# Which queue carries the first gate weights: exchanging the queues of two opening loads in a fused attention and gated-MLP kernel

## The chip, the cores and the metric

The kernel runs on one core of one Trainium2 chip. The metric is the device time of one execution in microseconds. Kernels are compared only within the same rounds.

## The reference

```python
x = A_x                                   # 2048 rows of 640, bf16
xn = _layernorm(x)
# A: queries xn @ wq, 32 heads of 192, the last 512 keys and values of a cache, softmax, @ wo
s = _A_ref(xn, A_k_cache, A_v_cache, A_wq, A_wo)
# B: sigmoid(xn @ w_gate) * (xn @ w_up), then @ w_down      (640 -> 1536 -> 640)
g = _silu(_B_ref(xn, B_w_gate, B_w_up, B_w_down))
return x + s * g
```

## The kernel before

The kernel computes the gate (B) first. It starts with row tiles of 128 rows: VectorE (DVE) takes the statistics of a tile and centres it, TensorE (PE) turns it through an identity matrix, ScalarE (ACT) copies the turned rows out of PSUM, and PE multiplies them with the first 512 columns of the gate weights, in five chunks of 128 rows of the weights. Seventeen dummy matmuls keep PE busy until the first rows are there (in the profile from 1.05 to 4.86 us; PE's first work on rows starts at 4.70).

These are the loads of the opening. `nc.sync` is SyncE's (SP) queue, `nc.scalar` is ScalarE's; a load that ScalarE issues waits for a fill of two columns (one 4-byte element, 0.06 us in the profile) of its own destination.

```python
def load_x(t, n, eng=nc.sync):
    x = xpool.tile([P, n, D], BF16, name=f"x_sb{n}", bufs=4 if n == 1 else 2)
    if eng is nc.scalar:
        nc.vector.memset(x[:, 0, 0:2], 0.0)
    eng.dma_start(x[:], xf[t * P:(t + n) * P, :].rearrange("(q p) d -> p q d", p=P))
    ...
nc.vector.memset(warm[:], 0.0)
nc.vector.memset(eps_t[:], eps)
load_x(0, 1)                                       # rows 0      SyncE    160 KB
load_x(1, 1, nc.scalar)                            # rows 1      ScalarE  160 KB
load_f(nc.sync, wg_sb, wg_r, 0, 4, 0, 3)           # gate 0 to 2 SyncE    384 KB
load_f(nc.scalar, wg_sb, wg_r, 0, 4, 3, NCD)       # gate 3, 4   ScalarE  256 KB
load_f(nc.sync, wu_sb, wu_r, 0, 4, 0, 3)           # up 0 to 2   SyncE    384 KB
load_x(2, 1)
load_f(nc.sync, wu_sb, wu_r, 0, 4, 3, NCD)
load_x(3, 1)
... # the rest of the weights and rows, all on SyncE
```

And this is the order in which PE consumes them (cut to the matmuls):

```python
dummy(17)
turn_pe(0, 0, 1); turn_pe(0, 1, 3, 2)
tile_half(0, 0, 0, 0, 0, 1)        # rows 0 x gate chunk 0
turn_pe(0, 3, NCD, 1)
tile_half(0, 0, 0, 0, 1, 3)        # rows 0 x gate chunks 1, 2
turn_pe(1, 0, 3)
tile_half(0, 0, 0, 0, 3)           # rows 0 x gate chunks 3, 4
turn_pe(1, 3, NCD, 2)
tile_half(1, 0, 1, 0)              # rows 1 x gate chunks 0 to 4
tile_half(0, 0, 0, 1)              # rows 0 x up: the first use of up weights
```

The softmax here doesn't subtract the row's maximum and nothing guards it: scores larger than these inputs give would overflow.

Of the kernel before, what the change touches and what calls it, by code (L numbers as in the profile page):

```python
# [15 lines left out]
def kernel(  # L16
# [13 lines left out]
    nc = tc.nc  # L30
    P = 128
    H2 = 64

    xf = A_x.flatten_outer_dims()
# [14 lines left out]
    NCD = D // P  # L49
# [36 lines left out]
    wg_r = B_w_gate.rearrange("(c p) f -> p c f", p=P)  # L86
# [56 lines left out]
    with ExitStack() as bctx:  # L143
# [5 lines left out]
        wg_sb = wB.tile([P, NCD, F], BF16, name="wg_sb")  # L149
# [6 lines left out]

        xt = {}

        def load_x(t, n, eng=nc.sync):

            x = xpool.tile([P, n, D], BF16, name=f"x_sb{n}", bufs=4 if n == 1 else 2)
            if eng is nc.scalar:

                nc.vector.memset(x[:, 0, 0:2], 0.0)
            eng.dma_start(x[:], xf[t * P:(t + n) * P, :].rearrange("(q p) d -> p q d", p=P))  # L165
            for i in range(n):
                xt[t + i] = x[:, i, :]

        def load_f(eng, w, r, f0, f1, c0=0, c1=NCD):
            eng.dma_start(w[:, c0:c1, f0 * P:f1 * P], r[:, c0:c1, f0 * P:f1 * P])  # L170

        nc.vector.memset(warm[:], 0.0)
        nc.vector.memset(eps_t[:], eps)
        load_x(0, 1)
        load_x(1, 1, nc.scalar)
        load_f(nc.sync, wg_sb, wg_r, 0, 4, 0, 3)
        load_f(nc.scalar, wg_sb, wg_r, 0, 4, 3, NCD)
        load_f(nc.sync, wu_sb, wu_r, 0, 4, 0, 3)
        load_x(2, 1)
        load_f(nc.sync, wu_sb, wu_r, 0, 4, 3, NCD)  # L180
        load_x(3, 1)
# [489 lines left out]
```

## Time and profile before

| | before |
|---|---|
| device time, median of the first runs | 922.05 us (921.91 to 922.11) |
| span of the profiled run | 920.4 us |
| PE busy | 913.7 us |
| gate chunks 3 and 4: issued, landed | 1.51, 6.90 us |
| PE's wait for them | 0.34 us |

PE's work in order of time (start, us busy, engine, line, operation, tiles, count; in brackets the idle time before it and what ended it).

```profile
5.51 0.39 PE L303 MATMUL bank<-wg_sb,xnT 128*128 128x512 bf16 x1 [0.16 <-ACT xnT L247]
...
6.95 0.59 PE L303 MATMUL bank<-wg_sb,xnT 128*128 128x512 bf16 x2 [0.34 <-DMA wg_sb<-in_B_w_gate_dram]
...
8.57 1.89 PE L303 MATMUL bank<-wu_sb,xnT 128*128 128x512 bf16 x8
```

The first row is gate chunk 0, the second gate chunks 3 and 4 after their wait, the third the first matmul with an up weight. I call the start of that third row (8.57 us) the **length of the opening**.

### The profile page before, as it was taken

The page shows a single profiled execution, that of the slowest core. Times are in us where ns is not written, and L with a number is a line of the kernel's source. Part 1 is how long each engine was busy: PE and PEld are TensorE (multiplying, and loading weights), DVE is VectorE, ACT ScalarE, POOL GpSimd, SP SyncE. Part 2 cuts the span into 40 slices and gives each one's busy share as a digit, 9 for nine tenths or more (in the row PEclk, how much of TensorE's full clock was granted, in tenths as well). Part 3 has the DMA queues.
Part 4 walks back from the last instruction along what each step waited for, and adds up shares of the span by engine and source line. Part 5 has one row for each costly group of instructions (what it writes and reads, how often), then busy time and mean ns, then how long its engine had stood idle before and what let it go on. Part 6 is the DMA issues. An engine that isn't in the chain of part 4 may idle for free.

```text
span 920.4 us, 24974 instructions
## 1 busy us (share of the span) xinstructions
PE 913.7 (99%) x11314; PEld 622.8 (68%) x11333; DVE 492.5 (54%) x987; ACT 303.1 (33%) x334; POOL 126.7 (14%) x147
## 2 busy tenths in 40 slices
PE   9999999999999999999999999999999999999998
PEld 4445455466868686767676777777776767686875
DVE  5452522545646464645555555545564646464667
ACT  4222222255142424233333333242414151515150
POOL 2000100001002000200120011001100111055813
PEclk9999999999999999999999999999999999999999
DMA  9830330116334434342425162516251614246435
GB/s 318 165 44 1 89 86 1 44 62 88 78 63 106 86 56 84 93 99 42 98 80 112 36 105 79 113 29 112 66 106 45 116 61 84 66 96 142 91 72 136
DMA packets 173642, 79.35 MB, mean 86 GB/s; under 512 B 149952, under 2 KB 169616, under 8 KB 173536
## 3 DMA queue, kind: packets, MB, share of 16 engines
q1 hardware_dynamic: 166928, 58.44, 32.1%
q0 software_dynamic: 5040, 17.89, 7.0%
q8 instruction: 88, 1.44, 0.7%
q10 hardware_dynamic: 1568, 1.43, 0.5%
q14 instruction: 18, 0.15, 0.1%
HBM read 39.45 MB, written 2.62 MB: 46 GB/s over the span
## 4 chain that ended last, share of the span: by engine, by line
PE 98%; DMA 1%; DVE 0%; issue 0%; ACT 0%; ACTq 0%; DVEq 0%
PE bank L531 22%; PE bank L457 21%; PE bank L479 19%; PE bank L439 18%; PE bank L261 8%; PE bank L273 6%; PE bank L303 3%; PE bank L405 1%; DMA wg_sb<-in_B_w_gate_dram 1%; PE bank L564 0%; DVE o_sb L509 0%; DVE gate L514 0%; ACT xnT L247 0%; PE bank L245 0%; ACTq L165 0%
## 5 line engine op out<-in xcount | busy, mean ns | idle before, releaser
L443 ACT ACTIVATE E<-bank 128x1024 bf16<-128x1024 f32 x256 | 255.4, 1022 | 456.6 <-PE bank L439 456.3
L457 PE MATMUL bank<-xnT,wq_sb 64*128 64x512 bf16 x1800 | 226.4, 376 | 0.0
L531 PE MATMUL bank<-wo_sb,oT 64*128 64x320 bf16 x2688 | 205.2, 296 | 0.0
L439 PE MATMUL bank<-qT,kT 64*128 64x512 bf16 x1536 | 200.9, 376 | 0.0
L479 PE MATMUL bank<-vbuf,E 64*128 64x193 bf16 x4096 | 195.3, 243 | 0.0
L479 PEld LDWEIGHTS <-E 64*128 64x128 bf16 x4096 | 178.8, 94 | 10.2 <-issue 0.3
L531 PEld LDWEIGHTS <-oT 64*128 64x128 bf16 (+1 forms) x2892 | 163.2, 94 | 30.7 <-issue 0.3
L464 DVE CAST qT<-bank 128x1024 bf16<-128x1024 f32 x90 | 110.2, 1225 | 128.5 <-PE bank L457 128.5
L457 PEld LDWEIGHTS <-wq_sb 64*128 64x128 bf16 x1800 | 106.1, 100 | 87.0 <-issue 0.4
L439 PEld LDWEIGHTS <-kT 64*128 64x128 bf16 x1536 | 88.1, 94 | 73.6 <-issue 0.3
L492 DVE TENSOR_TENSOR o_st<-bank,rden 128x768 bf16<-128x768 f32 x128 | 122.5, 957 | 4.4
L546 DVE TENSOR_TENSOR acc<-bank,acc 128x640 f32<-128x640 f32 x96 | 79.1, 824 | 20.2 <-PE bank L531 20.2
L118 POOL DMA_DIRECT2D vbuf<-in_A_v_cache_dram x28 | 21.1, 755 | 309.2 <-PE bank L479 306.3
L462 DVE COPY seen<-bank 128x2 f32<-128x2 f32 x90 | 14.3, 159 | 79.3 <-PE bank L457 79.3
L491 DVE RECIPROCAL rden<-bank 128x4 f32<-128x4 f32 x128 | 23.4, 183 | 60.6 <-PE bank L479 59.5
L273 PE MATMUL bank<-wd_sb,hT 128*128 128x128 bf16 (+1 forms) x377 | 52.4, 298 | 0.4
L273 PEld LDWEIGHTS <-hT 128*128 128x128 bf16 x384 | 29.7, 98 | 23.1
L261 PE MATMUL bank<-xnT,wg_sb 128*128 128x512 bf16 x176 | 44.5, 379 | 0.2
L261 PE MATMUL bank<-xnT,wu_sb 128*128 128x512 bf16 x177 | 44.6, 379 | 0.2
L267 DVE TENSOR_TENSOR hT<-bank,sig 128x512 bf16<-128x512 f32 x36 | 24.8, 690 | 37.1 <-ACT sig L264 37.1
L264 ACT ACTIVATE sig<-bank 128x512 bf16<-128x512 f32 x36 | 21.5, 597 | 55.8 <-PE bank L261 52.7
L110 POOL COPY k_perm<-k_st 128x768 bf16<-128x768 bf16 x32 | 25.6, 828 | 77.3 <-DMA k_st<-in_A_k_cache_dram 77.3
(52 smaller groups left out, 379.3 us busy)
## 6 DMA issues: line engine op xcount, KB each, us to landing
wo_sb<-in_A_wo_dram SPq DMA_DIRECT2D x7, 960.0 KB, 5.6
wq_sb<-in_A_wq_dram POOLq DMA_DIRECT2D x7, 960.0 KB, 6.0
k_st<-in_A_k_cache_dram POOLq DMA_DIRECT2D x14, 384.0 KB, 5.9
vbuf<-in_A_v_cache_dram POOLq DMA_DIRECT2D x28, 192.0 KB, 4.1
row<-in_A_x_dram SPq DMA_DIRECT2D x16, 160.0 KB, 2.4
oT<-o_st SPq DMA_TRANSPOSE x128, 3.2
x_sb<-in_A_x_dram SPq DMA_DIRECT2D x3, 640.0 KB, 9.4
wd_sb<-in_B_w_down_dram SPq DMA_DIRECT2D x1, 1920.0 KB, 13.9
```

Of the source, the lines that this page charges most:

```text
L110: nc.gpsimd.tensor_copy(kp[:, pr, :, :, i * H2:(i + 1) * H2], kst[:, i, :, :].rearrange("p c (i j) -> p c j i", j=DJ),)
L261: nc.tensor.matmul(bank[k][:, half, 0:r1 - r0], lhsT=w[:, c, f * P:(f + 1) * P], rhs=xnT[:, b, c, r0:r1], start=(c == 0), stop=(c == NCD - 1))
L273: nc.tensor.matmul(wide(k)[:, d0:d1], lhsT=hT[b][:, f, q * P:(q + 1) * P], rhs=wd_sb[:, f, d0:d1], start=(f == 0), stop=(f == NF - 1))
L303: nc.tensor.matmul(bank[k][:, half, :], lhsT=xcT[:, c, t * P:(t + 1) * P], rhs=w[:, c, fg * FT:(fg + 1) * FT], start=(c == 0), stop=(c == ...
L439: nc.tensor.matmul(bank[k][:, i, :], lhsT=kT[r, pr, j, c * P:(c + 1) * P], rhs=q[r, pr * DJ + j, :], start=(j == 0), stop=(j == DJ - 1))
L443: nc.scalar.activation(E[u, pr][:, c, :, :], bank[k][:], AF.Exp, scale=scale_qk)
L457: nc.tensor.matmul(bank[k][:, half, :], lhsT=wq[r, c, col:col + DJ * (P - 1) + 1:DJ], rhs=xnT[r, b, c, :], start=(c == 0 and not second), ...
L464: nc.vector.tensor_copy(qT[u][:, 2 * m:2 * m + 2, :], bank[k][:])
L479: nc.tensor.matmul(o4[:, q, 0:DH + 1], lhsT=e[r, c, h % 2, q * P:(q + 1) * P], rhs=vbuf[r, h, c, 0:DH + 1], start=(turn == 0 and qq == 0 a ...
L492: nc.vector.tensor_tensor(o_st[u][:, :, h * DH:(h + 1) * DH], o4[:, :, 0:DH], rden[:].to_broadcast([P, TQ, DH]), ALU.mult)
L531: nc.tensor.matmul(res[:, half, :], lhsT=oT[u][r, cc, q * P:(q + 1) * P], rhs=wo[r, cc, half * HD:(half + 1) * HD], start=(turn == 0 and c ...
L546: nc.vector.tensor_tensor(cols(acc[:, t, :]), res, cols(acc[:, t, :]), ALU.add)
```

## The change

The intent: the first two row tiles go out one after the other on SyncE's queue, and gate chunks 0 to 2, which are needed first, go out on ScalarE's at the same moment. A fill of 352 columns of their destination holds ScalarE's issue back so that the rows are ahead. Chunks 3 and 4 move to SyncE's queue, in front of the up weights.

```diff
-        def load_x(t, n, eng=nc.sync):
+        def load_x(t, n):
             x = xpool.tile([P, n, D], BF16, name=f"x_sb{n}", bufs=4 if n == 1 else 2)
-            if eng is nc.scalar:
-                nc.vector.memset(x[:, 0, 0:2], 0.0)
-            eng.dma_start(x[:], xf[t * P:(t + n) * P, :].rearrange("(q p) d -> p q d", p=P))
+            nc.sync.dma_start(x[:], xf[t * P:(t + n) * P, :].rearrange("(q p) d -> p q d", p=P))
...
         nc.vector.memset(eps_t[:], eps)
+        nc.vector.memset(wg_sb[:, 0, 0:352], 0.0)
         load_x(0, 1)
-        load_x(1, 1, nc.scalar)
-        load_f(nc.sync, wg_sb, wg_r, 0, 4, 0, 3)
-        load_f(nc.scalar, wg_sb, wg_r, 0, 4, 3, NCD)
+        load_x(1, 1)
+        load_f(nc.scalar, wg_sb, wg_r, 0, 4, 0, 3)
+        load_f(nc.sync, wg_sb, wg_r, 0, 4, 3, NCD)
```

## The prediction

> **What bounds the kernel now.** I read four views, from the whole to the opening. First the busy shares of the page, because a change of the opening can only matter as much as the engine that sets the end lets it.
>
> ```profile
> span 920.4 us, 24974 instructions
> PE 913.7 (99%) x11314; PEld 622.8 (68%) x11333; DVE 492.5 (54%) x987; ACT 303.1 (33%) x334; POOL 126.7 (14%) x147
> ```
>
> TensorE (PE) is busy 913.7 of 920.4 us, so all of the time without matmuls is 6.7 us. Second, the busy time by stretches says where these 6.7 us lie: of the first 20 us PE is busy 18.10, so 1.9 us are idle there; from 20 to 915 us only 0.94 us are idle (80 - 79.53 and 815 - 814.53), and the last 5.4 us hold 3.8 us of the tail (the last rows and their store), which the change leaves alone. The change touches only the first ten microseconds. It can therefore take out at most a part of 1.9 us, and 1.05 of these are the time before the first dummy matmul, which waits for the fill of its own tile and not for a load.
>
> Third, what PE waited for in the first 12 us (engine and line, who released it, total us, times, longest):
>
> ```profile
> PE bank L195 <- DVE x_sb L164: 1.0, 1, 1.0
> PE bank L303 <- DMA wg_sb<-in_B_w_gate_dram: 0.3, 1, 0.3
> PE bank L303 <- ACT xnT L247: 0.3, 2, 0.2
> ```
>
> One wait of 0.34 us (0.3 here, 0.34 in the timeline, between 6.61 and 6.95) is for gate weights; two of about 0.16 us are for turned rows copied out of PSUM by ScalarE (ACT). Fourth, the chain that ended last, in order of time (start, us, what), names which transfer that was:
>
> ```profile
> 1.05 0.43 ACTq L165
> 1.48 0.03 issue
> 1.51 5.39 DMA wg_sb<-in_B_w_gate_dram
> 6.90 0.04 issue
> 6.95 0.59 PE bank L303 x2
> ```
>
> The transfer issued at 1.51 from ScalarE's queue is the second part of the first gate weights (chunks 3 and 4 of 5, 256 KB). It lands 5.39 us after its issue, at 6.90. From there the chain is PE work, apart from two copies by ACT of 0.50 us that hold PE for 0.15 us each. So what this opening pays to the loads is 0.34 us, and the change is aimed at that transfer.
>
> Why does 256 KB take 5.39 us? Queue q1 is SyncE's (SP), q10 is ScalarE's. The DMA view for 2.4 to 5.2 us, and then for 5.2 to 6.6 us (packets, MB, share of 16 engines):
>
> ```profile
> q1 hardware_dynamic: 509, 0.50, 58.8%
> q10 hardware_dynamic: 388, 0.40, 41.3%
> ...
> q1 hardware_dynamic: 412, 0.43, 90.9%
> q10 hardware_dynamic: 28, 0.03, 5.9%
> ```
>
> ScalarE's queue has only the second x row tile (160 KB) and these weights: 416 KB, 416 packets with the completions. By 5.2 us 388 of them have gone; the last 28 need another 1.4 us, beside 412 of SyncE's. The packet records show more: the transfers were served nearly one after the other in order of issue (x0 from 1.6 us, x1 from 2.4, weights 0 to 2 from 2.8, weights 3 and 4 from 4.0, first up weights from 4.7), 14 of the 16 completions of weights 3 and 4 are there by 5.3 us, and two come at 6.46 and 6.54. On two DMA engines the rest of this transfer shared the time with the next transfers of the other queue, the up weights, which nobody needs before 8.57 us. That, not volume, is the wait.
>
> [...]
>
> **The change part by part.** The arithmetic, the order on PE, ACT and POOL after the issues, and the bytes are unchanged. SP issues one transfer more, ACT one less.
>
> *The fill.* The one-column fill of x1 (0.06 us) goes; one of 176 elements comes. From two rows, 1 element at 59 ns and 128 at 165 ns, a further element costs (165-59)/127 = 0.83 ns, so 59 + 175 x 0.83 = about 0.20 us. It starts at 0.95 as its predecessor did and ends at about 1.16. DVE next works at 3.22, so it costs nothing itself. ACT, which began 0.04 us after the end of the old fill (1.01 to 1.05), issues at about 1.20.
>
> *The issues.* Before, SP issues at 0.73, 1.19, 1.66, 2.18: a pace of about 0.47. After: x0 0.73, x1 1.19, weights 3 and 4 at 1.66, first up weights at about 2.15, each later one 0.47 later than before. ACT: weights 0 to 2 at 1.20, as good as the 1.19 they had. In order of issue: x0, x1, weights 0 to 2, weights 3 and 4, up. That is the order of before, with the queues exchanged. That SP's later issues slip costs nothing while the DMA engines have a backlog, and they have: from 2 us on their share is 0.90 to 1.10.
>
> *Weights 3 and 4.* The transfer now stands before the up weights in the same queue[...]. The 14 engines in order say 5.3 us for its last completion; landing was 0.36 us after that before (6.54 to 6.90), so about 5.7. Needed at 6.61: the wait of 0.34 goes, with 0.9 to spare.
>
> *Weights 0 to 2.* Last completion 4.51 before, landing at 1.19 + 3.8 = 5.0; needed at 5.51. If the order of service holds, still about 5.0; 0.5 to spare. It is now these that sit in ScalarE's queue, with weights 3 and 4 behind them in the other: what happened to the one may happen to the other.
>
> *x0 and x1.* x0 is ahead of all as before: landing about 3.15, and the first normalised piece at 4.69, where the 17 dummies (until 4.86) end anyway. x1 landed at 1.05 + 2.4 = 3.45; DVE reaches it at 4.55. Behind x0 in one queue it should land at 3.5 to 3.6: hidden.
>
> *What comes next if PE is 0.34 earlier.* Up weights landed at 1.66 + 5.9 = 7.6, needed at 8.23; their second part at 2.71 + 6.0 = 8.7, needed at about 9.4. x2 landed at 7.98, the last DVE piece before PE's turning is ready at 9.47 (9.15 + 0.32), and PE would ask for it at 10.08 - 0.34 = 9.74: 0.27 to spare. The same bytes stand before x2 as before, so it comes when it came. The two ACT waits stay, as they are between PE and ACT alone.
>
> **Sum:** minus 0.34 us of wait, plus 0 for the fill, plus 0 for the issues: -0.34, all of it carried to the end because nothing between 20 and 915 us waits for a clock other than PE's. For a chance that the exchange bites somewhere I keep 0.30: 922.05 - 0.30 = 921.75 us.
>
> **The rivals.**
> 1. *The late engine changes sides.* Weights 0 to 2, 24 packets on each DMA engine, are alone in ScalarE's queue while SyncE's has weights 3 and 4 and up weights behind. If two engines interleave as before, the landing goes from 5.0 to as much as 6.2. PE then starts the first gate matmul at 6.2 instead of 5.51, does what took from 5.51 to 6.61 (1.10 us) until 7.3, and begins chunk 3 there instead of at 6.95: a loss of about 0.35, so 922.4. For it: the same two queues, the same kind of neighbour. Against: the wait behind these weights was short in the old trace, since all their completions came within 0.5 us (4.03 to 4.51). I give it one in five; break-even is a landing at 5.85.
> 2. *ScalarE's issue overtakes x1.* The two issues are only about 0.01 us apart (1.19 and 1.20), on a fill whose length I worked out. If weights 0 to 2 are served first, x1 comes after them, near 4.5, lands about 4.9, and DVE starts its statistics 0.35 later than 4.55. PE's turn of x1 (6.28, its input ready at 6.03) slips by about 0.1: the gain shrinks to 0.2, so 921.85. For it: the near tie. Against: the fill has plainly been sized to hold this order.
> 3. *Something else was just behind.* If x2 or the up weights come 0.3 later, because SP issues them 0.47 later, PE loses the 0.34 again at 8.2 or 9.7, and the time is 922.05. Against: the backlog of the DMA engines.
>
> **Range and chances.** Some 55% for a gain of 0.2 to 0.5, 25% for about nothing, 20% for a loss of up to 0.4. The three runs of before span 0.20 us, so half of that is to be added at each side. That gives 921.3 to 922.3 as eight in ten. Two per cent would be 18 us, ten times all the idle time of the opening: faster 0.01, same 0.98, slower 0.01.
>
> **What would show it right or wrong.** Right: the waits of PE in the first 12 us have no line for the gate weights; the gate weights from ScalarE land at about 5.0, those from SyncE by 6; the first matmul with an up weight starts near 8.2; PE's busy time in the first 20 us is up by 0.3. Rival 1: a wait of PE for the gate weights before 6.2. Rival 2: DVE waits for x a second time before 5 us. Rival 3: a wait near 8 to 10 us that was not there. Wrong altogether: a difference that doesn't lie in the first 20 us.

What no trace or run of this case shows has been cut out of this text and of three of the expectations below; the cuts are marked. They take no term out of the sum: it came to minus 0.34 us for the wait and 0 for the fill and the issues, of which the author kept 0.30, so 922.05 - 0.30 = 921.75 us. What the argument needs of the cuts stands as follows:

- A landing followed the last of the 16 completions that the packet records have for a transfer: chunks 3 and 4 of the kernel before had 14 by 5.3 us and the last at 6.54, and landed at 6.90; in the changed kernel the last of chunks 0 to 2 came at 4.92, and they landed at 5.33.
- That the fill of 352 columns has 176 elements was an estimate from the warm tile, whose 256 columns show as 128 elements of uint32; the changed kernel's trace has a fill of 176.
- That chunks 3 and 4, in one queue with the up weights, would not share with them was an assumption. The landing of 5.7 us rests on it, and it is not shown.

The records do not name the DMA engine of a packet. Where these texts speak of a late engine, a late completion, one of the 16, is what was seen. And what the expectations call theory or rival is a guess put to the test, not a finding. For the two late completions of the kernel before the records show a little more: from 5.6 us the rest of the transfer goes in two trains, each with a packet every 0.085 us that takes 0.046 us, so that about half of the time was left to other packets.

## The result

The changed kernel took 921.67 us (median of 4, 921.55 to 921.80), the kernel before 921.98 us in the same rounds (median of 4, 921.80 to 922.11). The ratio, the mean time of one kernel's fast runs over that of the other's in the same rounds and so not quite the ratio of these medians, is 0.9997 with a 95% interval of 0.9979 to 1.0014. By the 2% measure it is the same time. The medians differ by 0.31 us. In these rounds and in two further sets of rounds, told below, the interval of the ratio includes 1; that the difference is real rests on the three sets together, in which all 13 runs of the changed kernel took 922.00 us or less, but only 8 of the 34 runs of the kernel before.

The page of the changed kernel, span and busy times:

```profile
span 919.8 us, 24974 instructions
PE 913.4 (99%) x11314; PEld 622.9 (68%) x11333; DVE 492.9 (54%) x987; ACT 303.1 (33%) x334; POOL 126.7 (14%) x147
```

PE does the same work. The span is 0.6 us shorter in this profile: half of that is idle time of PE (6.4 us instead of 6.7), the other half is its busy time. What PE waited for in the first 12 us (engine, line, releaser, total us, times, longest):

```profile
PE bank L194 <- DVE warm L169: 1.0, 1, 1.0
PE bank L302 <- DMA wg_sb<-in_B_w_gate_dram: 0.2, 1, 0.2
PE bank L302 <- ACT xnT L246: 0.2, 1, 0.2
```

There is still a line for gate weights, but it is another wait. The chain that ended last, in order of time, names the transfer:

```profile
1.00 0.20 DVE wg_sb L172
1.20 0.02 issue
1.22 4.11 DMA wg_sb<-in_B_w_gate_dram
5.33 0.04 issue
5.37 0.38 PE bank L302
```

The fill ends at 1.20, ScalarE issues chunks 0 to 2 at 1.22, and they land 4.11 us later, at 5.33. PE, whose other input was ready, starts the first gate matmul on them. Chunks 3 and 4 are no longer in the chain. The DMA view for 2.4 to 5.2 us shows ScalarE's queue (q10) with all of its 400 packets gone; in the view for 5.2 to 6.6 us SyncE's queue is the only one with data:

```profile
q1 hardware_dynamic: 460, 0.47, 55.8%
q10 hardware_dynamic: 400, 0.39, 45.4%
...
q1 hardware_dynamic: 478, 0.49, 104.6%
```

The 28 packets that were late before have no counterpart in ScalarE's queue. For chunks 3 and 4, now in SyncE's, the view can't tell, since it doesn't separate the transfers of one queue. Counted in order in the packet records, 14 of their 16 completions are there by 5.39 us and two come at 5.61 and 5.88, so a shorter tail seems to be left. PE's work in order of time:

```profile
5.37 0.38 PE L302 MATMUL bank<-wg_sb,xnT 128*128 128x512 bf16 x1 [0.20 <-DMA wg_sb<-in_B_w_gate_dram]
...
6.33 0.61 PE L302 MATMUL bank<-wg_sb,xnT 128*128 128x512 bf16 x2
...
7.04 1.25 PE L302 MATMUL bank<-wg_sb,xnT 128*128 128x512 bf16 x5
...
8.13 1.89 PE L302 MATMUL bank<-wu_sb,xnT 128*128 128x512 bf16 x8
```

The opening is 8.13 us long instead of 8.57, 0.44 less. Chunk 0 starts 0.14 earlier. From there to chunks 3 and 4 (the second row) it takes 0.96 us instead of 1.44, which is 0.48 less, more than the 0.34 us that the view put down as idle. The ends of PE's instructions are modelled: here chunks 3 and 4 start 0.21 us after the turn in front of them (6.12 to 6.33), while that turn is still shown busy. Before, the same turn started at 6.28, so chunks 3 and 4 could have started at 6.49, and the wait until 6.95 was worth 0.46 us. From chunks 3 and 4 to the up weights it takes 1.80 instead of 1.62: a part is given back. PE is now early enough that the rows of the second tile, which ACT copies out of PSUM from 6.49 to 6.98, come just before the matmuls that read them (7.04, the third row). So 0.14 + 0.48 - 0.18 makes the 0.44.

### The profile page after: what moved, and what is told of

It is laid out like the page before. It is cut to its first block, busy times and chain, and to the rows that moved or that the text cites. A ratio compares the mean times of both kernels' runs of the same rounds, so it can differ in the third digit from the quotient of the medians.

```text
span 919.8 us, 24974 instructions
## 1 busy us (share of the span) xinstructions
PE 913.4 (99%) x11314; PEld 622.9 (68%) x11333; DVE 492.9 (54%) x987; ACT 303.1 (33%) x334; POOL 126.7 (14%) x147
## 3 DMA queue, kind: packets, MB, share of 16 engines
q8 instruction: 88, 1.44, 0.7%
## 4 chain that ended last, share of the span: by engine, by line
PE 99%; DMA 0%; DVE 0%; issue 0%; ACT 0%; DVEq 0%
PE bank L530 22%; PE bank L456 21%; PE bank L478 19%; PE bank L438 18%; PE bank L260 8%; PE bank L272 6%; PE bank L302 3%; PE bank L404 1%; DMA wg_sb<-in_B_w_gate_dram 0%; PE bank L563 0%; DVE o_sb L508 0%; DVE gate L513 0%; ACT xnT L246 0%; PE bank L244 0%; DVEq L665 0%
```

## The experiments

My theory: the gain comes from gate chunks 3 and 4, of which the last 28 packets went after 5.2 us beside 412 of the other queue, the up weights, with two late completions, and which now stand before the up weights in one queue. The rivals: the gain is a lucky draw of the landings; it comes from the rows; or the hold does nothing. Twelve runs were made, in three sessions on three chips, all correct. The table has the landings that each profile shows (issue plus time to landing; two neighbouring issues of SyncE are shown as one, so the second rows' and some others are good to 0.1 us), PE's longest wait for gate weights, and the length of the opening.

| kernel | rows 1 land | gate 0 to 2 | gate 3, 4 | PE's wait | opening | profiled run | run minus opening | mean minus before's mean, same rounds (runs of each) |
|---|---|---|---|---|---|---|---|---|
| before | 3.5 | 5.0 | 6.9 | 0.34 | 8.57 | 922.16 | 913.59 | |
| before_again | 3.4 | 4.9 | 6.7 | 0.28 | 8.32 | 921.94 | 913.62 | -0.08 (5, 9) |
| changed | 4.5 | 5.3 | 6.3 | 0.20 | 8.13 | 921.55 | 913.42 | -0.29 (4, 4) |
| after_again | 3.7 | 5.2 | 6.0 | 0 | 8.45 | 921.87 | 913.42 | -0.42 (4, 7) |
| after_third | 4.0 | 5.0 | 6.0 | 0 | 8.16 | 921.88 | 913.72 | -0.93 (5, 9) |
| b_weights_sync | 3.7 | 5.6 | 6.4 | 0.59 | 8.43 | 922.19 | 913.76 | -0.33 (4, 7) |
| b_weights_again | 3.6 | 5.4 | 6.1 | 0.21 | 8.46 | 922.10 | 913.64 | -0.85 (5, 9) |
| b_x1_sync | 3.6 | 6.3 | 6.4 | 1.31 | 9.10 | 922.50 | 913.40 | +0.32 (4, 7) |
| no_hold | 5.4 | 5.6 | 6.2 | 0.34 | 9.04 | 922.65 | 913.61 | +0.37 (4, 7) |
| hold_176 | 4.5 | 5.3 | 6.1 | 0 | 8.20 | 921.64 | 913.44 | -0.82 (5, 9) |
| hold_512 | 3.7 | 5.6 | 6.0 | 0.35 | 8.44 | 922.12 | 913.68 | -0.74 (5, 9) |
| hold_704 | 3.4 | 7.3 | 7.0 | 2.36 | 11.50 | 924.99 | 913.49 | +1.89 (5, 9) |
| all_sync | 3.5 | 6.0 | 6.7 | 0.88 | 10.44 | 923.89 | 913.45 | +1.04 (5, 9) |
| after_split | 4.1 | 4.3 (0), 7.2 (1, 2) | 7.0 | 1.18 | 9.64 | 923.36 | 913.72 | +1.11 (5, 9) |

The column "run minus opening" is the time of the profiled run minus its opening. It lies between 913.40 and 913.76 in all fourteen profiles, while the openings differ by 3.4 us. So the time of each of these kernels is its opening plus a constant, to within 0.36 us: nothing after the first up weight hides or repeats the larger costs of the opening. That was assumed in the prediction and is measured here. For the gain itself, 0.3 us, the measure is too coarse: the openings of before (8.57, 8.32) and of the changed kernel (8.13, 8.45, 8.16) overlap, so the size of the gain is read from the means in the last column.

### The changed kernel again: after_again and after_third

The code is unchanged.

> The changed kernel once more, to see how far its opening repeats. Theory (the order of the transfers in the two queues sets the opening): gate chunks 0 to 2 land at 5.2 to 5.5 us and PE's first wait for them is 0.1 to 0.3 us, the second x rows land at 4.2 to 4.6, and the first matmul of the second weight group starts at 15.8 (before: 16.25). Rival (the landings are scatter from run to run): one of these is off by more than 0.4 us. Time 0.2 to 0.4 us under before.

> The changed kernel a third time, with five rounds, for the size of its gain: the two sessions so far gave 0.31 and 0.43 us under before by the medians, with scatter of 0.2 to 1.1 us. Theory (the gate wait of about 0.3 us near 6.6 is gone and nothing as large took its place): mean 0.2 to 0.5 us under before; no wait of PE for gate chunks 3 and 4; chunks 0 to 2 land at 5.2 to 5.4. Rival[...]: mean within 0.15 us of before.

Means: 921.87 against 922.29, and 921.74 against 922.67. Together with the first session the thirteen runs of the changed kernel lie between 921.55 and 922.00, and its mean is under that of before in all three sessions, by 0.29, 0.42 and 0.93 us (the last is outside the 0.2 to 0.5 that I had expected). None of its three profiles has a wait of PE for chunks 3 and 4. The landings are not as firm as I had expected: the second rows came at 4.5, 3.7 and 4.0, chunks 0 to 2 at 5.3, 5.2 and 5.0. In after_again the second rows are more than 0.4 us off, which by the rule set beforehand is the rival's point, and the second weight group started at 16.14 instead of 15.8. In after_again the opening is 8.45 though PE has no wait for weights at all, and PE's view in order of time says why:

```profile
5.47 0.60 PE L302 MATMUL bank<-wg_sb,xnT 128*128 128x512 bf16 x1 [0.17 <-ACT xnT L246]
```

The first gate matmul took 0.60 us, where it took 0.38 in the first profile. PE ran at half rate at the start of the profiles, and the change came at another place in each of those read. In the profile of the kernel before, dummies of 256 columns start 0.213 us apart, and from 5.5 us on matmuls of 512 columns start 0.216 us apart; its clock record has full rate from 5.41 us. The seventeen dummies take 3.81 us in most profiles (all at half rate) but 3.57 in after_third and 3.32 in b_weights_sync, and by the clock records packed with the traces full rate came at 5.1, 5.9 and 4.2 us in the three profiles of the changed kernel. With 8.45 against 8.13 us this is a draw of some 0.3 us in an opening. It is why one profile against one profile could not have decided this.

### The kernel before against itself: before_again

> The kernel before once more, against itself: how wide is the scatter of times (0.2 us in the first runs, 1.1 us in the last seven), and are the two late engines of gate chunks 3 and 4 there each time? Theory (late engines are a property of that order): chunks 3 and 4 land at 6.4 us or later again and PE waits for gate weights 0.1 us or more between 6 and 7 us. Rival (one bad draw in the first profile): they land by 6.0 and there is no wait. Ratio 1.000 within 0.0003.

```profile
6.70 0.59 PE L303 MATMUL bank<-wg_sb,xnT 128*128 128x512 bf16 x2 [0.28 <-DMA wg_sb<-in_B_w_gate_dram]
```

The wait for chunks 3 and 4 is there again, 0.28 us before chunk 3, with a landing at 6.7 us. It is there in both profiles of that order, so it was not one bad draw. The number of late completions differs: in the packet records twelve of the 16 completions are there by 5.16 us, and four come between 5.49 and 6.29, where the first profile had two. Against itself the ratio is 1.000. The scatter is much wider than the first three runs said: 921.79 to 922.93 here, 922.05 to 923.42 on the chip of the third session. The first rows landed at 3.0 here and at 3.2 in the first profile, and in the changed kernel at 3.0, 3.2 and 3.1: that the first profile of the changed kernel starts chunk 0 0.14 us earlier lies within this scatter and is not counted to the change.

### One part alone, the weights: b_weights_sync and b_weights_again

```diff
-        load_f(nc.scalar, wg_sb, wg_r, 0, 4, 3, NCD)      # in the kernel before
+        load_f(nc.sync, wg_sb, wg_r, 0, 4, 3, NCD)
```

> One part alone: as before, the second x rows stay on ScalarE's queue, but gate chunks 3 and 4 go out on SyncE's, right behind chunks 0 to 2. Theory (the 0.34 us wait came from the two late engines on which these chunks shared with the up weights of the other queue): no wait of PE for gate weights, chunks 3 and 4 land by 6.0, x1 at 3.4 to 3.6, chunks 0 to 2 at about 5.0; first matmul with an up weight near 8.2, the time 0.3 us under before. Rival (the gain of the change came from the first x rows landing 0.2 us earlier, since the second are no longer beside them): x0 lands at 3.2 as before and the gain is under 0.1 us.

> The one part alone again: second x rows still on ScalarE's queue, all first gate weights on SyncE's. Theory (putting chunks 3 and 4 into the queue of the up weights is the whole of the gain, the rest of the change is not needed): mean within 0.15 us of the changed kernel's in the same rounds and 0.2 us or more under before. Rival (its chunks 0 to 2, which landed at 5.6 with a wait of 0.59 us last time, are a lasting loss): they land at 5.5 or later again and the mean lies 0.15 us or more above the changed kernel's.

This single word gives 0.33 us where the whole change gave 0.42, and 0.85 where it gave 0.93. The wait for chunks 3 and 4 is gone in both profiles. The expectation failed in its detail: chunks 3 and 4 landed at 6.4 and 6.1, not by 6.0, and PE now waits for chunks 0 to 2, whose landing moved from 5.0 to 5.6 and 5.4:

```profile
5.67 0.38 PE L303 MATMUL bank<-wg_sb,xnT 128*128 128x512 bf16 x1 [0.59 <-DMA wg_sb<-in_B_w_gate_dram]
```

So the main part is shown: putting chunks 3 and 4 in the queue of the up weights removes the wait, and by the means it is nearly all of the gain (clear of the scatter in the second of the two sessions; the openings of the two profiles, 8.43 and 8.46, lie between those of before). Why it works is shown less far. The same edit has SyncE issue the first up weights at 2.17 instead of 1.66 us, and no run delays them alone, so whether the order within one queue or the later competitor matters stays untested. Whether the rest of the change adds the remaining 0.1 us can't be told from this scatter.

### The other part alone, the rows: b_x1_sync

```diff
+        nc.vector.memset(wg_sb[:, 3:5, 0:512], 0.0)       # in the kernel before: hold for chunks 3 and 4
+        nc.vector.memset(wg_sb[:, 3, 0:512], 0.0)
         load_x(0, 1)
-        load_x(1, 1, nc.scalar)
+        load_x(1, 1)
```

> The other part alone: the second x rows on SyncE's queue behind the first; gate chunks 0 to 2 stay on SyncE's behind them; chunks 3 and 4 stay on ScalarE's, held by two fills until about 1.75 us so that they still come after chunks 0 to 2. Theory: chunks 3 and 4 keep their late engines (landing 6.5 to 7), PE still waits for them 0.2 us or more, and the gain is under 0.15 us. Rival (x0 earlier is what counts): x0 lands at about 3.0 and the gain is 0.2 us or more.

No gain: 0.32 us above before. But the expectation was wrong about the place. Chunks 3 and 4, issued at 1.96 (the two fills took longer than I had reckoned), landed at 6.4, and chunks 0 to 2, pushed back to SyncE's third issue at 1.65, landed only at 6.3. PE waited 1.31 us for chunks 0 to 2. So this run doesn't say what the rows alone are worth: with them on SyncE's queue the first weights came third there, and that place is too late for them. The two late completions of chunks 3 and 4 did not stay either: their completions are spread over 5.09 to 5.98 us.

### The hold: no_hold, hold_176, hold_512, hold_704

```diff
-        nc.vector.memset(wg_sb[:, 0, 0:352], 0.0)         # in the changed kernel
+        nc.vector.memset(wg_sb[:, 0, 0:2], 0.0)           # no_hold
+        nc.vector.memset(wg_sb[:, 0, 0:176], 0.0)         # hold_176
+        nc.vector.memset(wg_sb[:, 0, 0:512], 0.0)         # hold_512
+        nc.vector.memset(wg_sb[:, 0, 0:352], 0.0)         # hold_704: the same fill twice
+        nc.vector.memset(wg_sb[:, 0, 0:352], 0.0)
```

> The changed kernel with a fill of one 4-byte element in place of 176, so that ScalarE issues gate chunks 0 to 2 at about 1.05 us, ahead of SyncE's issue of the second x rows at 1.19. Theory (the DMA engines serve by order of issue): the weights go first, land near 4.6, and x1 lands after 4.7; DVE waits for x1, PE for its turned rows, and the gain over before shrinks to 0 to 0.2 us. Rival (the queues are served alternately whatever the order, the hold is without effect): all landings within 0.2 us of the changed kernel's (3.0, 4.5, 5.3, 6.25) and the same time.

> The changed kernel with the fill done twice, so that ScalarE issues gate chunks 0 to 2 at about 1.43 us instead of 1.22, still ahead of SyncE's chunks 3 and 4 at 1.65. Theory (order of issue sets order of service; the near tie at 1.19 and 1.22 let x1 spread to 4.5 in one profile and 3.65 in the other): x1 lands by 3.8, chunks 0 to 2 at 5.2 to 5.5, the same time as the changed kernel within 0.2 us. Rival (each 0.2 us of hold is paid by the chunks): they land at 5.5 to 5.7 and the time is 0.2 us more than the changed kernel's.

> The changed kernel with a fill of 512 columns (256 elements, about 0.27 us), so that ScalarE issues at about 1.29 us: between the changed kernel's 1.22 and the 1.53 of the double fill, which cost 2 us. Theory[...]: between the two, chunks 0 to 2 land at 5.4 to 6.5, time 0 to 1.5 us above the changed kernel's. Rival (only the order of issue counts, and 1.53 was too near 1.65): the same as the changed kernel within 0.2 us.

> The changed kernel with a fill of 176 columns (88 elements, about 0.13 us), so that ScalarE issues at about 1.15 us, just ahead of SyncE's second x rows at 1.19. Theory (order of issue sets order of service): like the kernel without a hold: the weights go first, x1 lands after 4.8, and the time is at or above before. Rival (the two are near enough that the DMA engines mix them[...]): like the changed kernel, x1 by 4.5, the time 0.2 to 0.5 us under before.

ScalarE issued at 1.05 (no_hold), 1.13, 1.22 (the changed kernel), 1.30 and 1.53 us. Without the hold the gate weights begin first (67 of their packets have gone by 3.2 us, when the first of the second rows goes), and from then on the two share (91 packets of ScalarE's queue and 30 of SyncE's from 3.3 to 3.7 us). Both are late: the weights land at 5.6, not at 4.6 as expected, and DVE's statistics of these rows (its second line here) start at 5.40 instead of 4.55, after 0.84 us of idle time.

```profile
3.14 0.89 DVE L202 BATCH_NORM_STATS2 st<-x_sb 128x6 f32<-128x320 bf16 x2 [2.13 <-DMA x_sb<-in_A_x_dram]
5.40 0.89 DVE L202 BATCH_NORM_STATS2 st<-x_sb 128x6 f32<-128x320 bf16 x2 [0.84 <-DMA x_sb<-in_A_x_dram]
```

The gain turns into a loss of 0.37 us (expected was a gain of 0 to 0.2), so the hold is needed. This profile also ran at half rate until 7.0 us (two matmuls took 0.99 us at 6.21), which hid a part of PE's wait: the first turn of the second rows could start only at 7.04, on rows that were ready at about 6.9. Between 1.13 and 1.30 it makes no difference that the rounds resolve: the means of hold_176, the changed kernel and hold_512 in the same rounds are 921.85, 921.74 and 921.93 (hold_512 so fits both of its expectations). My expectation for hold_176 was wrong: issued at 1.13, before the start of SyncE's second issue at 1.2, the weights still did not overtake the rows.

The double fill is another matter. For 0.31 us of hold more, chunks 0 to 2 land 2.0 us later, at 7.3. The DMA view of hold_704 for 4.0 to 5.2 us shows the two queues side by side in equal parts:

```profile
q1 hardware_dynamic: 231, 0.23, 54.4%
q10 hardware_dynamic: 213, 0.21, 49.0%
```

Here the chunks did not come before SyncE's chunks 3 and 4 (issued at 1.65) but shared the time with SyncE's queue, in which these and then the up weights were issued. But even sharing alone doesn't make 7.3: 14 of the 16 completions are there by 5.34 us, and two come at 6.40 and 6.91. The view for 5.4 to 7.0 us shows the rest:

```profile
q1 hardware_dynamic: 546, 0.56, 101.4%
q10 hardware_dynamic: 21, 0.02, 3.8%
```

This is the picture of the kernel before again, two late completions of ScalarE's transfer beside SyncE's up weights, now for the chunks that are needed first: rival 1 of the prediction come true. Both expectations were wrong: the theory's, that 0.12 us ahead in the order of issue is enough, and the rival's, that the cost is the hold itself. And the wait costs more than its length. PE's view in order of time, and then the busy times by stretches, in which the last column but two is PE's granted clock:

```profile
7.33 0.59 PE L303 MATMUL bank<-wg_sb,xnT 128*128 128x512 bf16 x1 [2.36 <-DMA wg_sb<-in_B_w_gate_dram]
7.71 0.42 PE L245 MATMUL bank<-ident,xn 128*128 128x128 bf16 x2
7.92 1.06 PE L303 MATMUL bank<-wg_sb,xnT 128*128 128x512 bf16 x2
...
7.00:8.00 1.00, 0.67 (x4) 0.40 (x4) 0.00 (x0) 0.00 (x0) 0.77 (x3) 0.64 1.09 353
8.00:9.00 1.00, 1.00 (x7) 0.45 (x5) 0.31 (x1) 0.38 (x1) 0.00 (x0) 0.50 1.05 337
9.00:10.00 1.00, 1.00 (x6) 0.45 (x5) 0.93 (x4) 0.49 (x1) 0.00 (x0) 0.50 1.09 358
10.00:11.00 1.00, 1.00 (x6) 0.56 (x5) 1.00 (x5) 0.38 (x1) 0.48 (x1) 0.66 1.09 351
```

Two matmuls take 1.06 us where they took 0.59, two turns 0.42 where they took 0.28. After a wait of 2.36 us PE is back at half rate (a granted clock of 0.50), and the granted clock says for how long: 0.72 us of the first stretch, two whole ones and 0.68 of the last (a mean of 0.64 is 0.72 at half rate), 3.4 us together. The clock records have full rate from 3.86, half rate from 7.27 and full rate from 10.68 us, 3.41 us apart each time; in the stretch before the drop PE was busy for its first 1.1 us. Its five runs are 922.66, 922.98, 924.99, 925.02 and 925.33, two groups some 2 us apart. Only one of them is profiled, so that the upper group is the one with half rate is likely but shown for that run alone.

### Everything in one queue: all_sync

```diff
-        nc.vector.memset(wg_sb[:, 0, 0:352], 0.0)         # in the changed kernel
-        load_f(nc.scalar, wg_sb, wg_r, 0, 4, 0, 3)
+        load_f(nc.sync, wg_sb, wg_r, 0, 4, 0, 3)
```

> The changed kernel with every opening load on SyncE's queue, no fill, nothing on ScalarE's. Theory (transfers of two queues that meet on late engines make the tails): with one queue no tail: x0 at 3.0 us, x1 at 3.4, gate chunks 0 to 2 at 4.9 to 5.2, chunks 3 and 4 at 5.7 to 6.0 though they are issued 0.45 us later than in the changed kernel; time 0.3 to 0.5 us under before, as good as the changed kernel. Rival (the second queue is needed to get the first weights out in time, as SyncE's pace of 0.47 us an issue is too slow): chunks 0 to 2 land at 5.6 or later, PE waits for them 0.3 us or more and the time is that of before.

The rival was right, and by more than it said: 1.04 us above before. Chunks 0 to 2 are SyncE's third issue, at 1.65 us, and land at 6.0. A tail is there even with one queue: by count, all 48 completions of the first three transfers could be there at 4.86 us, and the landing came 1.15 us later, where ScalarE's transfers in the other runs landed 0.3 to 0.6 us after their last completion. So a completion was probably late here too; that is an estimate from these counts. The busy times by stretches (PE, PEld, DVE, ACT, POOL, then PE's granted clock, the DMA share and GB/s) show a hole:

```profile
3.00:3.50 0.50, 0.50 (x4) 0.38 (x3) 0.46 (x2) 0.00 (x0) 0.00 (x0) 1.00 0.55 131
3.50:4.00 0.50, 0.50 (x4) 0.32 (x3) 0.47 (x3) 0.00 (x0) 0.00 (x0) 1.00 0.85 258
```

In the changed kernel the same two stretches move 219 and 339 GB/s, at a DMA share of 0.84 and 0.97 instead of 0.55 and 0.85. Chunks 0 to 2 go out 0.43 us later, at 1.65 instead of 1.22, behind two other issues of the one queue, which come one every 0.47 us; they land 0.7 us later, at 6.0 instead of 5.3. The wait of 0.88 us comes with half rate again: two matmuls take 1.06 us at 6.65 and again at 7.82, full rate begins only at 9.8 us by the clock record, and the opening is 10.44. The granted clock of 1.00 in the view above (and in every microsecond of the first twelve) is no measurement here: the record begins with the first change, at 9.8 us, and the view fills in 1.00 before it. In hold_704, where half rate came back after a first change, it reads 0.50. Its runs too lie in two groups, 922.27 and 922.48 against 923.88 to 924.21.

### A smaller first transfer: after_split

```diff
-        load_f(nc.scalar, wg_sb, wg_r, 0, 4, 0, 3)        # in the changed kernel
+        load_f(nc.scalar, wg_sb, wg_r, 0, 4, 0, 1)
+        load_f(nc.scalar, wg_sb, wg_r, 0, 4, 1, 3)
```

> The changed kernel with gate chunk 0 as a transfer of its own ahead of chunks 1 and 2, both on ScalarE's queue. Theory (in the changed kernel the first gate matmul is held by the landing of chunks 0 to 2 at 5.2 to 5.35, its other input being ready at 5.1 to 5.3): chunk 0 lands at about 4.4, PE has no wait for gate weights before the second chunk, and the gain over the changed kernel is 0 to 0.15 us. Rival (an issue more on ScalarE and one more completion move the rest back): chunks 1 and 2 land at 5.6 or later, PE waits there, and the time is 0.1 to 0.3 us above the changed kernel's.

Chunk 0 does land early, at 4.3, as the theory said. But chunks 1 and 2, now issued after it at about 1.6, together with SyncE's chunks 3 and 4, land at 7.2, and PE waits 1.18 us there. It costs 1.11 us. Three late completions of 16 are in the packet records again (6.16, 6.21 and 6.82 us, the others by 5.69). As in hold_704 and b_x1_sync, a transfer on ScalarE's queue was issued at about the same time as a large one on SyncE's, or after it (at 1.6, 1.53 and 1.96 us, SyncE's at 1.65 each time), and both landed late: at 7.2 and 7.0 here, 7.3 and 7.0 in hold_704, 6.4 and 6.3 in b_x1_sync. That the two queues were served side by side is seen in the DMA view of hold_704 (231 against 213 packets); for the other two no such view was read.

## Why the prediction was right, and where not

The time was predicted as 921.75 us and came as 921.67 us; the wait of 0.34 us was named as the term to go, and it went. By its own steps:

- **Weights 3 and 4**: right in what goes, though not shown in why. In none of three profiles does PE wait for them, and moving them alone gives nearly the whole gain. The size of the slack was wrong: they land at 6.3, 6.0 and 6.0, not 5.7, and PE, who is earlier, asks for them at 6.33 in the first profile. Less than 0.1 us is spare there, not 0.9.
- **The fill and the issues**: right. The fill took 0.20 us, ScalarE issued at 1.22 (1.20 predicted), SyncE at 1.65 and 2.12 (1.66 and 2.15), and the later issues cost nothing (in the first 12 us PE waited for weights once, the 0.20 us for chunks 0 to 2).
- **Weights 0 to 2**: off in size. Landings of 5.3, 5.2 and 5.0 against 5.0 predicted. In the first PE waited 0.20 us for them, but no late completions caused it: ScalarE's end at 4.9 us there. Rival 1 did not happen in this kernel; hold_704 and after_split show it, with landings of 7.3 and 7.2 instead of the 6.2 that it reckoned with.
- **x0 and x1**: x1 landed at 4.5, 3.7 and 4.0 instead of 3.5 to 3.6. It was hidden in all three profiles, and rival 2 (ScalarE overtakes) did not happen; no_hold shows what it would have cost, some 0.8 us against the changed kernel (0.37 above before against 0.42 below), not the 0.1 that the rival reckoned with.
- **"Their second part ... needed at about 9.4"**: a slip. The fourth up matmul is three steps of 0.216 us after 8.57, at 9.22, and with PE 0.34 earlier at 8.88: 0.2 us of spare behind the landing at 8.7, not 0.7. It cost nothing, as that part landed at 8.5 in the changed kernel and was asked for at 8.78.
- **"So what this opening pays to the loads is 0.34 us"**: mis-sized. The wait was worth 0.46 us in the first profile and, by the same reading, 0.39 in before_again (turn at 6.10, so ready at 6.31, started at 6.70), because the idle time in the view begins only at a modelled end.
- **"The two ACT waits stay"**: failed: one more comes up, and it costs. Without the wait for weights PE reaches the second tile's rows early. From chunks 3 and 4 to the up weights it takes 1.80, 1.79 and 1.79 us in the three profiles of the changed kernel, and 1.62 in both of before. This new limit, the path of the second rows through DVE, PE and ACT, gives back 0.17.
- **Sum and scatter**: 0.39 to 0.46 gained less 0.17 given back is 0.22 to 0.29, so the predicted 0.30 came out of two errors that nearly cancel. The prediction took its scatter from three runs that span 0.20 us; over the later sessions the kernel before spans 1.8 us (921.66 to 923.42 in all its 34 runs) and the changed one 0.45 (13 runs). The gain by the means of three sessions is 0.29, 0.42 and 0.93 us, so 0.30 sits at its lower edge.
- **Missed altogether**: PE's half rate. In two profiles a wait in the first ten microseconds came together with slow matmuls after it (1.06 us for two instead of 0.59): 0.88 us in all_sync, 2.36 us in hold_704. Waits of 1.31 us in b_x1_sync and 1.18 us in after_split did not (0.59 us for two), so it is no rule. None of the rivals had it. Rival 1 gave 922.4 for its case; hold_704, whose profile shows that case, took 922.66 to 925.33.

What stays open: why a few completions come late (two to four of 16 in before, before_again, hold_704 and after_split); whether the later issue of the up weights would do without the change of queue; why the kernel before scatters so much more on some chips (only two of its executions are profiled, both with the wait near 0.3 us); and at which lead, between 1.30 and 1.53 us, ScalarE's weights begin to share with SyncE's. No version was found that is faster than the changed kernel beyond the scatter; hold_176 and b_weights_again are as good within 0.12 us.

## What to carry to other kernels

When two queues feed an opening, try to put each transfer in front of, and not beside, the one that is needed later: what hurt here was a needed transfer that was still under way beside an unneeded one of the other queue (waits of 0.34 us in the kernel before and of 2.36 us in hold_704). Order of issue can be tuned with a short fill, but look for the plateau (here 1.13 to 1.30 us) and stay clear of its edges, since both sides cost more than the tuning gained (0.37 us above before at 1.05 us, 1.89 us above it at 1.53). And before reading tenths of a microsecond out of one pair of profiles, repeat the old kernel and check that time minus opening is a constant.
